# Softmax's 1e-9 by a sum over a pair, and the four-batch products spread over 18 steps with their loads later

## The chip, the cores and the metric

The kernel runs on one core of a Trainium2 chip. The metric is the device time of one execution in microseconds (us); the kernel before takes 1392.96 us (median of three runs, 1392.74 to 1393.12).

## The reference

Attention over 8 batches, 8 heads, 576 positions and head size 64, with 32 memory slots, and behind it a mixture of four dense experts over the 4608 resulting rows. All is float32.

```python
a = softmax(phi, over the 32 slots)              # per batch and head: 576 x 32
k_m, v_m = a^T k, a^T v                          # 32 x 64
scores = (q k_m^T) / sqrt(64)
scores = scores - max(scores); attn = exp(scores)
attn = attn / (sum(attn) + 1e-9)                 # the 1e-9 that is changed
x = (attn v_m), heads side by side               # 4608 x 512
p = domain_probs / (sum(domain_probs) + 1e-9)
out = sum over e of p[:, e] * (relu(x w1[e]) w2[e])   # w1: 512 x 1024, w2: 1024 x 512
```

## The kernel before

Every float32 matrix is split into a high and a low part, and a product is three TensorE passes (high·high, high·low, low·high). x itself is never formed: `v_m` is multiplied into `w1` first ("vw", 256 x 1024 for a batch and an expert), and `relu(attn · vw)` is the hidden layer.

Batches go in pairs ("groups" k = 0 to 3). For k = 0 and 1 the work runs in steps numbered s: 128 steps (`PAIR`) for a group, 32 (`STEPS`) for each of its four experts, the first 16 for the even batch (odd = 0) and the others for the odd one. Each 16 are two halves of the batch's rows by eight chunks j of the hidden layer. A step calls, in this order, `accumulate()`, `run_plan(s)`, `first(s + 2)` and `second(s)`. `first` (lines 641 to 643) multiplies `attn` by vw for the step after next; it reads tile `vw[k, e, odd, j // 4, g]`, g = 0 and then 1, so chunks 0 to 3 need the pieces with fh = 0 and chunks 4 to 7 those with fh = 1. `second` (lines 674 to 676) multiplies the hidden chunk by `w2`. From step 256 (`BEGIN`) on, groups 2 and 3 run in another form (`unit`, line 1002).

`run_plan(s)` emits what the tables at the top of the file put at step s: splits of weights, parts of the attention of later batches, and these:

- `units_four`: for expert e and half fh it computes the rows of vw for four batches at once (`four_mm`, line 579), splits the result into a tile `vst` (line 584 on ScalarE, 585 on VectorE; a ring of three buffers, `KVS`) and stores it to memory as `vwd` from GpSimd's queue (`to_memory`, line 567). `FOUR_AT[fh][hp]` is the step, counted from the start of the expert before, at which the weights of pair hp are taken; its two products follow 2 and 3 steps later (`FOUR_LAG`). The table serves the fourth expert (e = 3) of batches 0 to 3, computed in steps 64 to 95, and the first (e = 0) of batches 4 to 7, in steps 224 to 255.
- `load_vw` (line 618): eight transfers of 128 KB on SyncE's (SP's) queue bring the pieces with one (odd, fh) of one expert back from memory. `VW_LOAD_AT[odd][fh]` is its step. It serves e = 3 of group 0, loaded from step 64 on, and of group 1, loaded from step 192 on.
- `load_w2` (line 186): in groups after the first the split `w2` comes back from memory, one chunk j of 512 KB per step from step 24 of the expert before (`W2_AGAIN`). Chunk j goes into the buffer that `second` leaves one chunk earlier.
- `write_v` (line 448): eight small transfers on SP that copy a batch's v into `vs`; for batch 7 in step 220.

Steps up to 36 are ordered by the compiler's scheduler; from step 36 each engine and each queue keeps the order in which the code emits its work. SP's queue is in order: a transfer whose wait isn't met holds all behind it.

The softmax of `attn` is `soft` (lines 490 to 493), 24 calls, all on VectorE: a sum over 32 slots, an addition of 1e-9, a reciprocal and the multiplication.

Of the kernel before, what the change touches and what calls it, by code (L numbers as in the profile page):

```python
# [9 lines left out]
F32 = mybir.dt.float32  # L10
# [3 lines left out]
AX = mybir.AxisListType  # L14
# [3 lines left out]
B, H, S, D, M = 8, 8, 576, 64, 32  # L18
N, DM, E, F = 4608, 512, 4, 1024
P = 128  # L20
# [12 lines left out]
AHEAD = 2  # L33

FREE = 36
VW_LOAD_AT = ((20, 25), (28, 32))
TURN = (0, 2, 1, 3)

FOUR = (3, 0)

FOUR_AT = ((6, 8, 10, 12), (14, 16, 18, 20))
FOUR_LAG = 2


# [39 lines left out]
def body(ctx: ExitStack, tc: tile.TileContext, qm, qt, kv, kvt, phi, prob, w1, w1d, w2, out):  # L84
    nc = tc.nc
    pool = lambda name, **k: ctx.enter_context(tc.tile_pool(name=name, bufs=1, **k))
    const, wp, work, att = pool("const"), pool("wp"), pool("work"), pool("att")
# [18 lines left out]
    def give(ps):  # L106
        tag, n, _ = lent.pop(id(ps))
        idle[tag].append(n)
# [4 lines left out]
    vts = [const.tile([P, NP, 2, P], F32R, name=f"vt{i}") for i in range(2)]  # L113
    for t in [vts[0].bitcast(F32)] + kT + [vts[1].bitcast(F32)]:
        nc.gpsimd.memset(t, 0.0)
    pt = const.tile([P, N // P, E], F32, name="pt")
    hm = work.tile([P, NJ, 2, P], F32R, name="hm")

# [136 lines left out]
    st = {}  # L255
# [196 lines left out]
    def tiles(t0):  # L452
        return (2, P) if t0 < 4 else (1, 64)
# [14 lines left out]
    def scores_max(b, t0):  # L468
        nt, n = tiles(t0)
        sc = st["sc", b, t0]  # L470
        scv = sc.rearrange("p i a (h m) -> p (i a h) m", m=M)[:n, :nt * H, :]
        mx = att.tile([P, 2 * H, 1], F32, name="mx", tag="mx", bufs=2)
        nc.vector.tensor_reduce(mx[:n, :nt * H, 0], scv, AX.X, ALU.max)
        at = att.tile([P, nt * H, M], F32, name="at", tag=f"at{t0}")
        av = at[:n, :nt * H, :]
        nc.vector.tensor_sub(av, scv, mx[:n, :nt * H].broadcast_to([n, nt * H, M]))
        give(sc)
        st["at", b, t0] = at

    def scores_exp(b, t0):  # L480
        nt, n = tiles(t0)
# [3 lines left out]
    def soft(b, t0):  # L485
        nt, n = tiles(t0)
        av = st["at", b, t0][:n, :nt * H, :]
        z = att.tile([P, 2 * H, 1], F32, name="z", tag="z", bufs=2)
        zv = z[:n, :nt * H]
        nc.vector.reduce_sum(zv[:, :, 0], av, AX.X)  # L490
        nc.vector.tensor_scalar_add(zv[:, :, 0], zv[:, :, 0], 1e-9)
        nc.vector.reciprocal(zv[:, :, 0], zv[:, :, 0])
        nc.vector.tensor_mul(av, av, zv.broadcast_to([n, nt * H, M]))

# [3 lines left out]
    def unit_scores(b, t0):  # L498
        def emit(q):
            scores_mm(b, t0, q)  # L500
            scores_max(b, t0)
            scores_exp(b, t0)
            soft(b, t0)
        return q_key(b, t0), emit
# [107 lines left out]
    def load_vw(k, e, odd, fh):  # L612
        b = 2 * k + odd
        for g in range(2):
            t = vw_tile(k, e, odd, fh, g)
            for h in range(4):
                r = slice(M * slot(b, h), M * slot(b, h) + M)
                nc.sync.dma_start(t[r].bitcast(F32), vwd[b // 4, e, fh, g, h][r])
# [85 lines left out]
    def at(s, unit):  # L704
        plan[s].append(unit if isinstance(unit, tuple) else (None, unit))
# [32 lines left out]
    def attention(b, s, written, scores, turns):  # L738
# [27 lines left out]
        for t0, n in zip((0, 2, 4), scores):  # L766
            at(n, (q_key(b, t0), lambda q, t0=t0: scores_mm(b, t0, q)))
            at(n + 1, lambda t0=t0: scores_max(b, t0))
            at(n + 2, lambda t0=t0: scores_exp(b, t0))
            at(n + 3, lambda t0=t0: soft(b, t0))  # L770
# [11 lines left out]
    for k in range(NG):  # L782
        for e in range(E):
# [19 lines left out]
            for fh in range(2):  # L803
                when, gap = (FOUR_AT_7, 2) if s >= BEGIN else (FOUR_AT, 1)
                for hp in range(NP if by_four and nk % 2 == 0 else 0):
# [4 lines left out]
                for odd in range(2 if by_four else 0):  # L810
                    when = VW_LOAD_AT if nk < SEVEN else VW_LOAD_7
                    at(s + when[odd][fh], lambda a=(nk, ne, odd, fh): load_vw(*a))
# [309 lines left out]
    with tc.manual_schedule():  # L1122
# [54 lines left out]
        kv_pick(0, 1)  # L1177
        scores_mm(0, 0, q, (2, 3))
        scores_max(0, 0)
        split_w1(w1g[0], 0, 1, gps)  # L1180
        write_vt_0(0, slice(1, 2))
# [4 lines left out]
        scores_exp(0, 0)  # L1186
        vw_out(pv[0], 0, 0, 0, 0, (0,))
        soft(0, 0)
        keep_warm(3)
        for hp in (1, 2):  # L1190
# [83 lines left out]
```

## Time and profile before

| | |
|---|---|
| time, median of 3 runs | 1392.96 us |
| profiled execution | 1392.14 us, span of its instructions 1390.3 us |
| PE (TensorE matmul) busy | 1362.0 us (98%) |
| DVE (VectorE) busy | 841.3 us (61%) |
| ACT (ScalarE) busy | 625.4 us (45%) |
| POOL (GpSimd) busy | 617.4 us (44%) |
| mean granted TensorE clock | 0.997 of full speed |
| HBM traffic over the span | 215 GB/s |

In the rows of the profile a number at the start is the time in us since the span began, the next one the duration; then come engine, line and operation, what is written `<-` what is read, and in square brackets how long the engine idled ahead of it and what ended that. Of a merged row (x4) the duration is that of all of them. SPq and POOLq are the queues from which these engines issue transfers.

### The profile page before, as it was taken

How to read it: one execution, taken by the hardware profiler on the slowest of the kernel's cores; microseconds unless marked ns; L12 is line 12 of the kernel's file. 1: busy time of each engine (PE TensorE's matmuls, PEld its weight loads, DVE VectorE, ACT ScalarE, POOL GpSimd, SP SyncE). 2: the span in 40 equal slices, each digit the busy share in tenths (PEclk: the TensorE clock that was granted, in tenths of full speed). 3: DMA queues.
4: the chain of work that ended last, by engine and by line, in shares of the span. 5: the costliest groups of instructions: out<-in, count | busy, mean ns of one | idle time of the engine just before them, and what ended most of it. 6: DMA issues, size and time to landing. Idle time of an engine off the chain costs nothing.

```text
span 1390.3 us, 25223 instructions
## 1 busy us (share of the span) xinstructions
PE 1362.0 (98%) x8894; PEld 1248.4 (90%) x8894; DVE 841.3 (61%) x1894; ACT 625.4 (45%) x1536; POOL 617.4 (44%) x652
## 2 busy tenths in 40 slices
PE   7999999999999999999999999999999999999998
PEld 6788888788888888889888998999999999999998
DVE  7875535446755365454434467777767666666666
ACT  6765555443345465463344354555543333333332
POOL 4400354745353424433144375677753334443432
PEclk9999999999999999999999999999999999999999
DMA  6742354897675364354598898899984866666661
GB/s 255 240 165 76 117 182 173 311 322 240 210 281 212 107 229 146 125 203 143 178 290 296 277 321 292 286 344 311 326 298 131 259 186 177 180 173 175 175 181 75
DMA packets 102029, 301.37 MB, mean 217 GB/s; under 512 B 24976, under 2 KB 26128, under 8 KB 101904
## 3 DMA queue, kind: packets, MB, share of 16 engines
q1 hardware_dynamic: 81168, 224.26, 51.9%
q0 software_dynamic: 19584, 71.31, 13.0%
q10 hardware_dynamic: 1152, 4.19, 0.7%
q8 instruction: 71, 1.16, 0.3%
q14 instruction: 54, 0.44, 0.1%
HBM read 213.46 MB, written 84.93 MB: 215 GB/s over the span
## 4 chain that ended last, share of the span: by engine, by line
PE 89%; DVE 4%; DMA 2%; issue 2%; ACT 1%; SPq 0%; POOL 0%; DVEq 0%; ACTq 0%; POOLq 0%
PE banks L1002 22%; PE banks L676 9%; PE banks L674 9%; PE banks L675 9%; PE banks L916 5%; PE banks L917 5%; PE banks L918 5%; PE banks L641 5%; PE banks L642 4%; PE banks L643 4%; PE banks L579 3%; PE banks L463 2%; PE banks L357 2%; DMA stage<-in_w 1%; PE banks L1040 1%
## 5 line engine op out<-in xcount | busy, mean ns | idle before, releaser
L1020 DVE SCALAR_TENSOR_TENSOR acc<-banks,pt,acc 128x256 f32<-128x256 f32 x416 | 200.0, 481 | 107.7 <-PE banks L1002 104.2
L160 POOL TENSOR_TENSOR w<-stage,w 128x512 fp32r<-128x512 f32 x134 | 177.0, 1332 | 188.7 <-ACT w L159 179.4
L655 DVE SCALAR_TENSOR_TENSOR h<-banks,h 128x256 fp32r<-128x256 f32 x256 | 107.3, 420 | 168.6 <-ACT h L653 111.4
L676 PE MATMUL banks<-w,h 128*128 128x512 f32 x512 | 201.2, 393 | 3.4 <-DVE h L655 3.4
L674 PE MATMUL banks<-w,h 128*128 128x512 f32 x512 | 201.9, 394 | 0.1
L675 PE MATMUL banks<-w,h 128*128 128x512 f32 x512 | 201.4, 393 | 0.0
L653 ACT ACTIVATE h<-banks 128x256 fp32r<-128x256 f32 x256 | 98.0, 384 | 199.8 <-PE banks L643 169.9
L641 PE MATMUL banks<-AT,vw 128*128 128x256 f32 (+1 forms) x512 | 156.6, 306 | 3.7 <-DVE h L655 1.8
L1002 PE MATMUL banks<-w,a 128*128 128x256 f32 x1080 | 154.4, 282 | 0.3 <-DVE acc L1020 0.2
L643 PE MATMUL banks<-AT,vw 128*128 128x256 f32 (+1 forms) x512 | 150.9, 295 | 1.2 <-DVE vw L556 1.2
L916 PE MATMUL banks<-AT,vw 128*128 128x256 f32 (+1 forms) x512 | 151.6, 296 | 0.0
L642 PE MATMUL banks<-AT,vw 128*128 128x256 f32 (+1 forms) x512 | 151.3, 296 | 0.0
L917 PE MATMUL banks<-AT,vw 128*128 128x256 f32 (+1 forms) x512 | 151.1, 295 | 0.0
L918 PE MATMUL banks<-AT,vw 128*128 128x256 f32 (+1 forms) x512 | 150.9, 295 | 0.0
L1002 PEld LDWEIGHTS banks<-w,a 128*128 128x128 f32 x1080 | 143.6, 188 | 4.8 <-issue 0.9
L983 POOL TENSOR_TENSOR vt<-ph,vt 128x512 fp32r<-128x512 f32 x64 | 84.1, 1314 | 107.3 <-ACT vt L982 78.3
L676 PEld LDWEIGHTS banks<-w,h 128*128 128x128 f32 x512 | 96.3, 188 | 25.8 <-DVE h L655 4.3
L346 POOL TENSOR_TENSOR kvs<-stage,kvs 128x512 fp32r<-128x512 f32 x58 | 75.4, 1317 | 93.2 <-ACT kvs L345 87.3
L641 PEld LDWEIGHTS banks<-AT,vw 128*128 128x128 f32 x512 | 96.8, 189 | 13.8 <-DVE vw L556 3.8
L674 PEld LDWEIGHTS banks<-w,h 128*128 128x128 f32 x512 | 96.4, 188 | 12.0 <-ACT h L653 0.4
L675 PEld LDWEIGHTS banks<-w,h 128*128 128x128 f32 x512 | 96.4, 188 | 10.9
L159 ACT CAST w<-stage 128x512 fp32r<-128x512 f32 x168 | 102.7, 619 | 4.5 <-DMA stage<-in_w 2.1
(149 smaller groups left out, 2985.4 us busy)
## 6 DMA issues: line engine op xcount, KB each, us to landing
w<-kw SPq DMA_DIRECT2D x93, 512.0 KB, 5.5
vwd<-vst POOLq DMA_DIRECT2D x80, 512.0 KB, 6.4
vw<-vwd SPq DMA_DIRECT2D x320, 128.0 KB, 6.0
w<-v SPq DMA_DIRECT2D x55, 512.0 KB, 5.6
stage<-in_w SPq DMA_DIRECT2D x44, 512.0 KB, 4.5
stage<-in_w1d SPq DMA_DIRECT2D x40, 512.0 KB, 5.3
stage<-in_kv SPq DMA_DIRECT2D x32, 512.0 KB, 4.3
kw<-w POOLq DMA_DIRECT2D x24, 512.0 KB, 5.6
```

What stands on the lines that cost most here:

```text
L160: eng.tensor_sub(dst[:, 1, :], raw, dst[:, 0, :].bitcast(F32))
L641: nc.tensor.matmul(ps, w[:, 0, f], at_t[:, g, 0, c], start=g == 0, stop=False)
L642: nc.tensor.matmul(ps, w[:, 0, f], at_t[:, g, 1, c], start=False, stop=False)
L643: nc.tensor.matmul(ps, w[:, 1, f], at_t[:, g, 0, c], start=False, stop=g == 1)
L674: nc.tensor.matmul(po[t], x[:, 0, :], w[:, 0, :], start=j == 0, stop=False)
L675: nc.tensor.matmul(po[t], x[:, 0, :], w[:, 1, :], start=False, stop=False)
L676: nc.tensor.matmul(po[t], x[:, 1, :], w[:, 0, :], start=False, stop=j == NJ - 1)
L916: nc.tensor.matmul(ps, w[:, 0, f], at_t[:, g, 0, c], start=g == 0, stop=False)
L917: nc.tensor.matmul(ps, w[:, 0, f], at_t[:, g, 1, c], start=False, stop=False)
L918: nc.tensor.matmul(ps, w[:, 1, f], at_t[:, g, 0, c], start=False, stop=g == 1)
L1002: nc.tensor.matmul(ps, a[:, l, jj], w[:, r, c], start=start and jj + i == 0, stop=jj == 1 and i == 2, skip_group_check=True,)
L1020: VE.scalar_tensor_tensor(a, src, p, a, ALU.mult, ALU.add)
```

## The change

```diff
-VW_LOAD_AT = ((20, 25), (28, 32))
+VW_LOAD_AT = ((20, 29), (28, 36))
...
-FOUR_AT = ((6, 8, 10, 12), (14, 16, 18, 20))
+FOUR_AT = ((6, 8, 10, 13), (15, 17, 20, 22))
...
+    guarded = const.tile([P, 2 * H, 2], F32, name="guarded")
+    nc.gpsimd.memset(guarded[:, :, 1], 1e-9)
...
-        st["at", b, t0] = at
+        st["at", b, t0], st["mx", b, t0] = at, mx
...
-        z = att.tile([P, 2 * H, 1], F32, name="z", tag="z", bufs=2)
-        zv = z[:n, :nt * H]
-        nc.vector.reduce_sum(zv[:, :, 0], av, AX.X)
-        nc.vector.tensor_scalar_add(zv[:, :, 0], zv[:, :, 0], 1e-9)
+        zv = st["mx", b, t0][:n, :nt * H]
+        nc.vector.reduce_sum(guarded[:n, :nt * H, 0], av, AX.X)
+        nc.vector.reduce_sum(zv[:, :, 0], guarded[:n, :nt * H], AX.X)
         nc.vector.reciprocal(zv[:, :, 0], zv[:, :, 0])
         nc.vector.tensor_mul(av, av, zv.broadcast_to([n, nt * H, M]))
```

The addition of 1e-9 becomes a second sum, over the pair (sum, 1e-9), into the tile that held the maximum. The sixteen products of one expert, one per step over 16 steps before, now have one step free behind the sixth and one behind the twelfth. Both loads of the pieces with fh = 1 come four steps later. The lines of the changed file are numbered two higher from line 115 or so on, and one higher behind `soft`.

The first place is SP's queue around step 217 to 222, where group 1 gets its fourth expert. `vwd` + five digits is a stored piece: batch set 0, expert 3, fh, g, and the head within g; `kw3j` is chunk j of the fourth expert's `w2`. Before:

```order
L186 DMA w2_6846<-kw31_3987 128x1024
L618 DMA vw_6848<-vwd03100_2966 32x1024
...
L618 DMA vw_6853<-vwd03113_3186 32x1024
L186 DMA w2_6881<-kw32_4013 128x1024
L186 DMA w2_6901<-kw33_4036 128x1024
L186 DMA w2_6918<-kw34_4067 128x1024
L618 DMA vw_6920<-vwd03000_2737 32x1024
...
L618 DMA vw_6925<-vwd03013_2934 32x1024
L448 DMA vs_5331<-vh_6883 64x2x32 x8
L186 DMA w2_6955<-kw35_4086 128x1024
L186 DMA w2_6977<-kw36_4108 128x1024
```

And after:

```order
L188 DMA w2_6830<-kw31_3977 128x1024
L188 DMA w2_6855<-kw32_4003 128x1024
L188 DMA w2_6875<-kw33_4026 128x1024
L188 DMA w2_6892<-kw34_4057 128x1024
L619 DMA vw_6894<-vwd03000_2733 32x1024
...
L619 DMA vw_6899<-vwd03013_2950 32x1024
L450 DMA vs_5320<-vh_6857 64x2x32 x8
L188 DMA w2_6929<-kw35_4076 128x1024
L619 DMA vw_6931<-vwd03100_2982 32x1024
...
L619 DMA vw_6936<-vwd03113_3212 32x1024
L188 DMA w2_6961<-kw36_4098 128x1024
```

The eight loads of the even batch's fh = 1 pieces stood ahead of chunk 2 of `w2`; now they stand behind chunk 5, the eight loads of the odd batch's fh = 0 pieces and the eight writes of `vs`.

The second place is PE's order in step 226, in which `first(228)` reads those pieces. Before:

```order
L676 MATMUL banks_72<-w2_6846,h_7010 128x512
L641 MATMUL banks_72<-AT_3431,vw_6848 128x256 [waits DMAHW6_49,DMAHW7_49,DMAHW5_49,DMAHW0_49]
L642 MATMUL banks_72<-AT_3431,vw_6848 128x256
L643 MATMUL banks_72<-AT_3431,vw_6848 128x256
L641 MATMUL banks_72<-AT_3431,vw_6853 128x256 [waits DMAHW3_49,DMAHW4_49,DMAHW2_49,DMAHW1_49]
```

And after:

```order
L677 MATMUL banks_72<-w2_6830,h_6994 128x512
L642 MATMUL banks_72<-AT_3416,vw_6931 128x256 [waits DMAHW3_49,DMAHW4_49,DMAHW2_49,DMAHW1_49]
L643 MATMUL banks_72<-AT_3416,vw_6931 128x256
L644 MATMUL banks_72<-AT_3416,vw_6931 128x256
L642 MATMUL banks_72<-AT_3416,vw_6936 128x256 [waits DMAHW6_49,DMAHW7_49,DMAHW5_49,DMAHW0_49]
```

PE's order has not moved: the matmul stands behind the `w2` chunk of step 225 in both, and waits for the four transfers of each tile.

The third place is VectorE's order around `soft` for batch 2, in step 98. Before:

```order
L655 SCALAR_TENSOR_TENSOR h<-banks,h 128x256 x2
L490 TENSOR_REDUCE z<-at 128x16
L491 TENSOR_SCALAR z<-z 128x16
L492 RECIPROCAL z<-z 128x16
L493 TENSOR_TENSOR at<-at,z 128x512
L655 SCALAR_TENSOR_TENSOR h<-banks,h 128x256 x2
```

And after:

```order
L656 SCALAR_TENSOR_TENSOR h<-banks,h 128x256 x2
L491 TENSOR_REDUCE guarded<-at 128x16
L492 TENSOR_REDUCE mx<-guarded 128x16
L493 RECIPROCAL mx<-mx 128x16
L494 TENSOR_TENSOR at<-at,mx 128x512
L656 SCALAR_TENSOR_TENSOR h<-banks,h 128x256 x2
```

One operation changes its kind; its place in the queue, ahead of the split of the hidden layer (`h`), stays. In steps up to 36 the scheduler, which counts the operations' costs, has also ordered a number of rows otherwise on every engine.

## The prediction

> **What bounds the kernel now.** I read the page first, then PE's waits, then the time lines of PE, VectorE, GpSimd and SP at the places where PE waits and where the change moves work.
>
> ```profile
> PE 1362.0 (98%) x8894; PEld 1248.4 (90%) x8894; DVE 841.3 (61%) x1894; ACT 625.4 (45%) x1536; POOL 617.4 (44%) x652
> PE 89%; DVE 4%; DMA 2%; issue 2%; ACT 1%; SPq 0%; POOL 0%; DVEq 0%; ACTq 0%; POOLq 0%
> ```
>
> PE is busy for 98% of the span and holds 89% of the chain that ended last. Its matmuls do not change, so the change can only pay or cost where PE waits: 28.3 us in all (1390.3 - 1362.0). Of PE's waits these are the longest behind the start:
>
> ```profile
> PE banks L676 <- DVE h L655: 3.4, 2, 2.0
> PE banks L579 <- ACT h L653: 2.5, 1, 2.5
> ```
>
> The columns are us in total, how often, and the longest. The 2.0 us is tied to the softmax, the 2.5 us to the four-batch products; I take each in turn, then the moved loads.
>
> **The sum over a pair.** All 24 additions of 1e-9, and three rows of the one that matters:
>
> ```profile
> L491 DVE TENSOR_SCALAR z<-z x24: 152/175/5192, 27.8 to 1062.7; 128x16 f32<-128x16 f32 x16, 64x8 f32<-64x8 f32 x8
> L490 DVE TENSOR_REDUCE z<-at x24: 399/676/686, 27.1 to 1062.3; 128x16 f32<-128x512 f32 x16, 64x8 f32<-64x256 f32 x8
> 334.44 5.19 DVE L491 TENSOR_SCALAR z<-z 128x16 f32<-128x16 f32 x1
> 334.10 5.49 POOL L160 TENSOR_TENSOR w<-stage,w 128x512 fp32r<-128x512 f32 x4
> 341.63 0.50 PE L676 MATMUL banks<-w,h 128*128 128x512 f32 x1 [2.03 <-DVE h L655]
> ```
>
> Sixteen numbers per partition take 175 ns as a rule, and 5192 ns once: from 334.44 to 339.63, while GpSimd ran four subtractions back to back until 339.59. The hidden layer's split stood behind it on VectorE, and PE idled 2.03 us for it. The sum in its place costs, by the two shapes of the other sums (399 ns for 256 elements, about 680 for 512: some 1.1 ns an element over about 120 ns), about 155 ns for 32 elements: 24 times nothing gained or lost. A sum over 512 elements never took over 686 ns in 24 executions, however busy GpSimd was, so I let the new one not wait. That removes PE's 2.03 us. Next in line is the multiplication, which reads two operands from SBUF; it has waited for GpSimd too:
>
> ```profile
> 850.78 1.68 DVE L493 TENSOR_TENSOR at<-at,z 128x512 f32<-128x512 f32 x1
> ```
>
> 1.68 us is its longest, so it slips in after one GpSimd operation. At 334.9 it would end by about 336.6 instead of 340.6, and the split in time. Term: -2.0 us (bounds: -2.0, and -0.3 if it waits as the addition did).
>
> The Trainium skill, SBUF — State Buffer, section Who interferes with whom, says that `tensor_scalar` can take a mode that needs the port pair shared with GpSimd, that `tensor_reduce` on trn2 never does, and that a two-input operation from SBUF contends with GpSimd's reads. The rows agree on the first two; by the third the wait could move to the multiplication, which is the second rival below.
>
> The constant's memset stands on GpSimd's queue at the start behind others and ahead of 3.8 us of idle time there; its cover is that idle time, and without it it would cost a fraction of a us. 0.
>
> **The products in 18 steps.** The wait of 2.5 us:
>
> ```profile
> 261.16 1.10 POOL L567 DMA_DIRECT2D vwd<-vst  x1
> 270.19 0.58 ACT L584 CAST vst<-banks 128x512 fp32r<-128x512 f32 x1 [7.52 <-DMA vwd<-vst]
> 271.65 0.47 PE L579 MATMUL banks<-w,vs 128*128 128x512 f32 x1 [2.53 <-ACT h L653]
> 272.40:275.80 3.40, 3.09 (x10) 2.80 (x11) 1.87 (x5) 2.29 (x7) 3.36 (x5) 0.50 0.64 123
> 275.90:279.30 3.40, 3.40 (x19) 2.94 (x18) 0.33 (x2) 0.60 (x2) 0.95 (x2) 1.00 1.01 401
> ```
>
> ACT waits 7.52 us for the first store, issued at 261.16, because the ring holds three pieces and this is the fourth. PE then stops ahead of the sixth product. The first six products keep their steps (6, 8 and 10 in the table are unchanged); the free steps come behind them. So this wait stays, with its price: 2.53 us and 3.4 us in which TensorE had half its clock (0.50 in the first window row, 1.00 in the next), worth 1.7 us. From there to 334 us PE does not wait, and it does not between 597 and 861 us, where the table's other use lies, so the free steps have nothing to remove. Sixteen products of two matmuls are the same work wherever they stand. Their stores end two steps later, which matters only to the loads below. Term: 0 (bounds -0.5 and +1, the size of PE's small waits).
>
> **The moved loads, first use (step 93).** `first(100)` in step 98 needs them.
>
> ```profile
> 318.01 0.35 SPq L145 DMA_DIRECT2D stage<-in_w  x1
> 334.45 0.28 PE L641 MATMUL banks<-AT,vw 128*128 128x256 f32 x1
> 313.48 4.14 SPq L618 DMA_DIRECT2D vw<-vwd  x8
> L618 SPq DMA_DIRECT2D vw<-vwd x320: 302/419/1489, 289.3 to 1331.9; - x160
> DMA to landing us min/median/max: 2.3/6.0/9.7
> ```
>
> SP now issues them behind the weights' load that went out at 318.01. Eight loads take SP 4.1 us (313.48) to about 6 and land 6.0 us after issue: 318.4 + 5.2 + 6.0 = 329.6, against a need at 334.45. Hidden, by 5 us. Ahead of it the last store must land, two steps later than before, at about 321. Term: 0.
>
> **The moved loads, second use (step 221).** Here steps take 2.1 us only:
>
> ```profile
> 688.40 0.28 PE L641 MATMUL banks<-AT,vw 128*128 128x256 f32 x1
> 700.96 0.28 PE L641 MATMUL banks<-AT,vw 128*128 128x256 f32 x1
> 701.32 0.28 PE L641 MATMUL banks<-AT,vw 128*128 128x256 f32 x1
> 709.31 0.31 PE L641 MATMUL banks<-AT,vw 128*128 128x320 f32 x1
> ```
>
> At 709.31 the width turns to 320: that is `first(232)`, step 230. Back by 2.09 us a step, step 226 begins at 700.96, where `first(228)` needs the tile with g = 0, and at 701.32 the one with g = 1; 688.40 is step 220. SP's queue meanwhile:
>
> ```profile
> 682.28 0.33 SPq L186 DMA_DIRECT2D w<-kw  x1
> 682.65 4.22 SPq L618 DMA_DIRECT2D vw<-vwd  x8
> 687.20 1.72 SPq L186 DMA_DIRECT2D w<-kw  x3
> 688.97 6.52 SPq L618 DMA_DIRECT2D vw<-vwd  x8
> 695.80 4.66 SPq L448 DMA_DIRECT2D vs<-vh  x6
> 699.50 2.67 SPq L448 DMA_DIRECT2D vs<-vh  x3
> 702.26 1.64 SPq L186 DMA_DIRECT2D w<-kw  x3
> 703.95 6.18 SPq L618 DMA_DIRECT2D vw<-vwd  x8
> ```
>
> (The two `vs` rows overlap by one of the eight.) Before, the loads in question went out at 682.65. In the new order they stand behind chunk 5 of `w2`, so behind everything down to 702.26. SP cannot run ahead of this: chunk 4 waits for the buffer that step 219 leaves at 688.4, and the queue after it is bound by its transfers. Worked out:
>
> - the odd batch's eight loads from 688.97: between 4.14 and 6.52 us; 1 MB less is under way ahead of them than before, so I take 4.2: 693.2
> - eight `vs` writes: 6.4 us before (695.80 to 702.2), at least eight times their shortest:
>
> ```profile
> L448 SPq DMA_DIRECT2D vs<-vh x64: 590/606/1420, 28.9 to 701.2; - x64
> ```
>
>   or 4.7; I take the middle, 5.6: 698.8
> - chunk 5: 0.4: 699.2
> - the eight loads: between 4.14 and 6.18, taken as 5.2: the last goes out by 704.4 and lands 6.0 later, at 710.4. The fourth, which ends the wait for g = 0, lands at 699.2 + 2.6 + 6.0 = 707.8.
>
> PE stops at 700.96 until 707.8, does three matmuls, and stops again until 710.4: 710.4 - 701.3 = 9.1 us. The least is 688.97 + 4.1 + 4.7 + 0.3 + 4.1 + 2.3 (the shortest landing) = 704.5, a loss of 3.2; the most is the old position, 702.6 + 6.2 + 9.7 = 718.5, a loss of 17.2. Both ends are past the need. A stop like this should halve the clock as the one of 2.53 us did: 3.4 us at 0.50 cost 1.7 (bounds 0 and 2.6, one and a half such stretches). The Trainium skill, TensorE: Matmul & The Clock Gate, Part 1, asks for an idle window of about 3.4 us before the clock drops; in the trace 2.53 us sufficed, and the measurement decides; a stop of 9 us meets either.
>
> Behind the stop PE has what it needs: chunks 6 and 7 go out after the loads but are due 8 us later than before, and the odd batch's other eight loads are due in step 242. Term: +9.1 + 1.7 = +10.8.
>
> **The scheduled steps up to 36.** PE waits there, as in
>
> ```profile
> 37.17 0.50 PE L676 MATMUL banks<-w,h 128*128 128x512 f32 x1 [1.37 <-DVE h L655]
> 49.87 0.39 PE L643 MATMUL banks<-AT,vw 128*128 128x256 f32 x1 [0.82 <-DVE vw L556]
> ```
>
> and rows change places around it. No row tells which way; the waits from 33 us on (1.37 + 0.82 and smaller) bound a gain at 2.6, a loss is taken as large. Term: 0.
>
> **Sum**: -2.0 + 9.1 + 1.7 = +8.8 us on the profiled execution of 1392.14 us (1.8 above its span) gives 1400.9. The median of the runs is 0.8 above that execution, 1392.96; on it 1401.8 us.
>
> **Rivals.**
> 1. The loads come in time after all (other side). Place: SP's queue from 688.4 to 701. It decides at the point where all eight have landed by 701.3, so the last must go out by about 695.3, before SP had begun the `vs` writes in the old trace (695.80). Speaking for it: the queue holds 1 MB less ahead of them. Against: even the shortest rows give 704.5. Then only the softmax counts: 1392.96 - 2.0 = 1391.0; with 0.8 us or more from the scheduled steps it would be faster by over 0.2% (2.8 us, about what a measurement tells from no change).
> 2. The loads are late and the softmax's wait moves to the multiplication, held until 339.6 as the addition was. For it: it has two inputs from SBUF, and 1.68 us shows that it waits. Against: in 24 executions it never waited for more than one operation. It ends 0.3 us earlier than before: 1401.8 + 1.7 = 1403.5.
> 3. The first use is late too: decided by SP reaching it 5 us later than 318.4. 3 us more: 1404.8.
>
> **Chances.** Forecast 0.70, rival 1 0.13, rival 2 0.12, rival 3 0.05. The range for 8 in 10: the low end, 1396.5, is the forecast with SP some 5 us quicker than taken; the high end, 1407, takes in rivals 2 and 3 and a loss of 14 us at step 226. Rival 1 lies outside below. Faster: 0.04 (rival 1 with luck at the start). Within 0.2%: 0.09 from rival 1 and 0.02 from the forecast's low tail, whose least sum is 3.2 - 2.0 = +1.2. Slower: 0.85.
>
> **What would show it.** In the trace after: no addition over GpSimd's chain near 334 us and no PE idle time at 341; the wait at 271 us as before, half clock behind it; PE idle at about 699 (701 less the 2.0) on its vw matmul, released by transfers `vw<-vwd`, in two pieces of some 7 and 2.5 us, and a window of clock 0.50; the eight loads leaving SP behind the `vs` writes, near 699 to 705. Wrong it would be if SP passed the `vs` writes before 692, if step 226 took other tiles than those, or if the start moved by more than 3 us.

## The result and the profile after

The changed kernel takes 1407.15 us (median of six runs, 1403.07 to 1408.55) against 1393.04 (1391.14 to 1395.85) for the kernel before on the same chip: a ratio of 1.0092, 95% interval 1.0077 to 1.0106, so 12.8 us slower by the ratio. The execution that the profile shows took 1405.31 us, its span 1403.4 us. The page's engine row, its chain of work that ended last, the clock in 40 slices, and the longest of PE's waits:

```profile
PE 1364.9 (97%) x8894; PEld 1250.5 (89%) x8894; DVE 836.8 (60%) x1894; ACT 625.5 (45%) x1536; POOL 618.0 (44%) x653
PE 87%; DVE 5%; DMA 3%; issue 2%; ACT 2%; POOL 1%; SPq 1%; ACTq 0%; DVEq 0%; POOLq 0%
PEclk9999999999999999999989999999999999999999
PE banks L642 <- DMA vw<-vwd: 10.0, 2, 8.9
PE banks L677 <- DVE h L656: 5.0, 3, 2.0
PE banks L580 <- ACT h L654: 0.7, 1, 0.7
```

PE's busy time grew by 2.9 us only (1364.9 - 1362.0), the time in which it is idle by 10.2. A wait for transfers `vw<-vwd` that was not there before, 10.0 us in two pieces, stands at the top, and one slice of the clock is no longer full. With the matmuls of both traces laid side by side by their place in PE's order (times of the kernel before), the changed kernel is 1.5 us behind at 46 us, 3.5 at 95 and 3.3 at 269; it is level again at 280 and still level at 700, 13.1 behind past step 226, and 13.2 at the end.

**Step 226.** SP's queue, PE, two windows (length, PE busy, PEld, DVE, ACT, POOL, then granted clock, share of DMA, GB/s), and the first matmul of `first(232)`:

```profile
682.31 6.64 SPq L188 DMA_DIRECT2D w<-kw  x4
689.00 4.88 SPq L619 DMA_DIRECT2D vw<-vwd  x8
693.98 6.36 SPq L450 DMA_DIRECT2D vs<-vh  x8
700.43 0.54 SPq L188 DMA_DIRECT2D w<-kw  x1
701.02 7.29 SPq L619 DMA_DIRECT2D vw<-vwd  x8
710.02 0.56 PE L642 MATMUL banks<-AT,vw 128*128 128x256 f32 x1 [8.87 <-DMA vw<-vwd]
712.15 0.58 PE L642 MATMUL banks<-AT,vw 128*128 128x256 f32 x1 [1.15 <-DMA vw<-vwd]
703.20:706.60 3.40, 0.00 (x0) 0.00 (x0) 0.00 (x0) 0.00 (x0) 0.00 (x0) 0.50 1.01 275
710.00:716.80 6.80, 5.63 (x18) 4.78 (x19) 0.42 (x1) 0.38 (x1) 0.00 (x0) 0.50 0.98 265
722.39 0.31 PE L642 MATMUL banks<-AT,vw 128*128 128x320 f32 x1
```

The loads that PE needs at 701.2 (710.02 - 8.87) leave SP from 701.02 to 708.31, behind the odd batch's loads and the eight `vs` writes. While PE is idle the clock falls to 0.50, and it is still 0.50 when PE is back: 5.63 us of work at half clock cost 2.8 us. The first matmul of `first(232)`, at 709.31 us in the profile before, starts at 722.39, so this place costs 13.1 us; the waits and the half clock are 12.8 of them.

**The softmax near 335 us.** The sum over the pair, GpSimd's four subtractions, the multiplication and PE:

```profile
334.52 0.18 DVE L492 TENSOR_REDUCE mx<-guarded 128x16 f32<-128x32 f32 x1
334.61 5.51 POOL L162 TENSOR_TENSOR w<-stage,w 128x512 fp32r<-128x512 f32 x4
335.03 5.65 DVE L494 TENSOR_TENSOR at<-at,mx 128x512 f32<-128x512 f32 x1
341.67 0.50 PE L677 MATMUL banks<-w,h 128*128 128x512 f32 x1 [1.98 <-DVE h L656]
```

The new sum does not wait. The multiplication behind it does, until GpSimd's chain is through, and PE idles 1.98 us where it idled 2.03.

**The products near 271 us.** GpSimd's first store, ScalarE's fourth split, and PE's sixth product:

```profile
264.42 1.09 POOL L568 DMA_DIRECT2D vwd<-vst  x1
271.64 0.58 ACT L585 CAST vst<-banks 128x512 fp32r<-128x512 f32 x1 [5.72 <-DMA vwd<-vst]
273.09 0.47 PE L580 MATMUL banks<-w,vs 128*128 128x512 f32 x1 [0.70 <-ACT h L654]
```

ScalarE went on 7.2 us after the issue of the store that it waits for (264.42 to 271.64), where it was 9.0 before (261.16 to 270.19). PE waits 0.70 us instead of 2.53, and the clock does not fall. The first use of the moved loads is hidden: SP issues them from 317.87 to 322.6, and PE does not wait for them.

### The profile page after: what moved, and what is told of

It reads as the page before. It is cut to its first block, busy times and chain, and to the rows that moved or that the text cites. A ratio compares the mean times of both kernels' runs of the same rounds, so it can differ in the third digit from the quotient of the medians.

```text
span 1403.4 us, 25226 instructions
## 1 busy us (share of the span) xinstructions
PE 1364.9 (97%) x8894; PEld 1250.5 (89%) x8894; DVE 836.8 (60%) x1894; ACT 625.5 (45%) x1536; POOL 618.0 (44%) x653
## 4 chain that ended last, share of the span: by engine, by line
PE 87%; DVE 5%; DMA 3%; issue 2%; ACT 2%; POOL 1%; SPq 1%; ACTq 0%; DVEq 0%; POOLq 0%
PE banks L1003 22%; PE banks L677 8%; PE banks L676 8%; PE banks L675 8%; PE banks L917 5%; PE banks L918 5%; PE banks L919 5%; PE banks L642 4%; PE banks L643 4%; PE banks L644 4%; PE banks L580 2%; PE banks L359 2%; PE banks L465 2%; DVE vw L557 1%; PE banks L1041 1%
```

## The experiments

The kernels of the first four ran together beside the kernel before at 1393.08 us, the next four beside 1393.22, the last two beside 1394.24; all are medians, and ratios are to those.

**1. The kernel before, with only the second use's loads later.** `VW_LOAD_AT` gets a pair for each expert so served; `nk` is 0 for group 0 and 1 for group 1.

```diff
-VW_LOAD_AT = ((20, 25), (28, 32))
+VW_LOAD_AT = (((20, 25), (28, 32)), ((20, 29), (28, 36)))
...
-                    when = VW_LOAD_AT if nk < SEVEN else VW_LOAD_7
+                    when = VW_LOAD_AT[nk] if nk < SEVEN else VW_LOAD_7
```

> The kernel before, with the four-step delay of the loads with fh = 1 for the second use alone (the fourth expert of group 1). Theory A (the loads stand behind the vs writes in SP's queue and reach step 226 too late; PE waits about 10 us and then works 4.7 us at half clock): 12 to 14 us slower than before, about 1406, with PE waiting 8 to 10 us on transfers vw<-vwd near 701 us. Theory B (the loss comes mostly from the start and the scheduled steps, which the softmax reorders, and the wait at step 226 is a part): 5 us slower or less.

Measured: 1407.89 us, ratio 1.0096 (1.0078 to 1.0113). PE around step 226, from that trace:

```profile
712.59 0.55 PE L641 MATMUL banks<-AT,vw 128*128 128x256 f32 x1 [6.86 <-DMA vw<-vwd]
715.00 0.58 PE L641 MATMUL banks<-AT,vw 128*128 128x256 f32 x1 [1.43 <-DMA vw<-vwd]
```

Both loads with fh = 1 of group 1 move, sixteen transfers; PE waits for the even batch's eight. This move alone makes the whole loss (1.0096 against 1.0092); side by side this place costs 11.8 us.

**2. The changed kernel, with the second use's loads back.**

```diff
-VW_LOAD_AT = ((20, 29), (28, 36))
+VW_LOAD_AT = (((20, 29), (28, 36)), ((20, 25), (28, 32)))
...
-                    when = VW_LOAD_AT if nk < SEVEN else VW_LOAD_7
+                    when = VW_LOAD_AT[nk] if nk < SEVEN else VW_LOAD_7
```

> The changed kernel, with the old load steps for the second use alone. Theory A: no wait at step 226, so 1392 to 1396, the kernel before within what differs at the start (+3.5 us in the profile) and at the four-batch products (-3.6 us). Theory B: it stays over 1400.

Measured: 1393.88 us, ratio 1.0005 (0.9991 to 1.0018); PE does not wait between 690 and 725 us. All that is left of the change, the sum over the pair, the 18 steps and the first use's later loads, comes to nothing that the interval (-1.3 to +2.5 us) tells from zero.

**3. Only the sum over the pair.** The kernel before with the edits of the softmax as in the change.

> The kernel before, with the sum over a pair alone. Theory A (the wait for GpSimd passes to the multiplication behind it): no gain, 1393 within 2 us, the multiplication of 5 to 6 us and PE's wait of 2 us near 341 us still there. Theory B (the multiplication was held by chance in the one profile): a normal multiplication of 0.7 to 1.7 us there and 1391. Theory C (the new order of the scheduled steps costs): 1396 or more, with the loss before 95 us.

Measured: 1396.05 us, ratio 1.0011 (1.0000 to 1.0023). No gain; the median is 3.0 us above that of the kernel before, more than Theory A's 2, and the interval just touches 1. The multiplication in that trace:

```profile
334.60 5.67 DVE L494 TENSOR_TENSOR at<-at,mx 128x512 f32<-128x512 f32 x1
```

It is held in both traces, so this is no chance of one execution, and PE idles 2.01 us behind it. Theory C, a loss in the scheduled steps, isn't excluded: this trace has one too (see the scheduled steps below).

**4. Only the products in 18 steps, with the first use's loads later.**

```diff
-VW_LOAD_AT = ((20, 25), (28, 32))
+VW_LOAD_AT = (((20, 29), (28, 36)), ((20, 25), (28, 32)))
...
-FOUR_AT = ((6, 8, 10, 12), (14, 16, 18, 20))
+FOUR_AT = ((6, 8, 10, 13), (15, 17, 20, 22))
...
-                    when = VW_LOAD_AT if nk < SEVEN else VW_LOAD_7
+                    when = VW_LOAD_AT[nk] if nk < SEVEN else VW_LOAD_7
```

> The kernel before, with the products in 18 steps and the later loads that they need for the first use, and the old loads for the second. Theory A (the wait at 271 us comes ahead of the free steps, and its size changes from run to run): 1393 within 2 us, a wait ahead of the sixth product of 0.5 to 3 us. Theory D (the free steps do remove it): 1389, without that wait.

Measured: 1394.26 us, ratio 1.0004 (0.9990 to 1.0019). The wait ahead of the sixth product, from the list of PE's waits and from ScalarE's rows:

```profile
PE banks L579 <- ACT h L653: 2.7, 1, 2.7
271.69 0.59 ACT L584 CAST vst<-banks 128x512 fp32r<-128x512 f32 x1 [7.73 <-DMA vwd<-vst]
```

It is as long as before, and 2.2 us in experiment 2, which has the 18 steps too; in experiment 3, which has not, it is 1.3. The wait follows the time from the store's issue to ScalarE's split: 9.2 us here, 8.8 in experiment 2, 7.9 in experiment 3, 7.2 in the profile of the changed kernel. So the 0.70 us there came with a quicker store in that one execution, not with the 18 steps.

**5. The changed kernel, with batch 7's `vs` writes four steps later,** so that the eight loads pass them on SP's queue.

```diff
-        at(written + 2, lambda: write_v(b, b < 4))
+        at(written + (6 if b == 7 else 2), lambda: write_v(b, b < 4))
```

> The changed kernel, with the eight writes of batch 7's v to vs four steps later (224, not 220), so that in SP's queue they stand behind the late loads instead of ahead. Theory A (the loads wait for their turn in SP's queue): the 6.4 us that the writes held the queue fall away, PE's wait at step 226 drops from 10.0 to about 4 us, and the time to 1398 to 1401. Theory E (the transfer engines are full there, and the order matters little): the wait drops by less than 2 us, and the time stays over 1404.

Measured: 1400.99 us, ratio 1.0055 (1.0039 to 1.0071), 6.2 us less than the changed kernel. SP and PE:

```profile
691.87 4.26 SPq L619 DMA_DIRECT2D vw<-vwd  x8
696.36 0.34 SPq L188 DMA_DIRECT2D w<-kw  x1
696.88 5.50 SPq L619 DMA_DIRECT2D vw<-vwd  x8
704.09 8.68 SPq L450 DMA_DIRECT2D vs<-vh  x8
704.95 0.36 PE L642 MATMUL banks<-AT,vw 128*128 128x256 f32 x1 [0.93 <-DMA vw<-vwd]
707.69 0.39 PE L642 MATMUL banks<-AT,vw 128*128 128x256 f32 x1 [2.15 <-DMA vw<-vwd]
```

Nothing of the loads themselves changed, only what stands ahead of them. The wait falls from 10.0 to 3.1 us (0.93 + 2.15); the difference of 6.9 is about what the eight writes held the queue for (6.36). Side by side this place costs 5.2 us instead of 13.1; that the medians differ by 6.2 and not by 7.9 stays open. The 3.1 us that are left fit the odd batch's loads, which still stand ahead (4.26 us), but no run takes these away.

**6. Experiment 1 with the eight late loads issued from ScalarE's queue.**

```diff
-                nc.sync.dma_start(t[r].bitcast(F32), vwd[b // 4, e, fh, g, h][r])
+                (nc.scalar if (k, odd, fh) == (1, 0, 1) else nc.sync).dma_start(t[r].bitcast(F32), vwd[b // 4, e, fh, g, h][r])
```

> The kernel before with the late loads of the second use, as in the run that was 0.96% slower, but the eight late ones issued from ACT's queue in the same step 221. Theory A: ACT reaches them within about 2 us of step 221 (690.5 us) and they land by about 701, so PE waits 0 to 2 us at step 226, and the time is 1392 to 1396. Theory E: with as many bytes under way they land as late as on SP's queue, and PE waits 5 us or more.

Measured: 1398.61 us, ratio 1.0031 (1.0019 to 1.0043). The time was missed. PE does not wait for the loads any more, but ScalarE, which computes on the same instruction stream, is held while it issues them:

```profile
690.49 7.07 ACTq L618 DMA_DIRECT2D vw<-vwd  x8
697.65 0.62 ACT L213 CAST sv<-raw 128x512 fp32r<-128x512 f32 x1 [6.80 <-DMA vw<-vwd]
698.60 0.50 PE L674 MATMUL banks<-w,h 128*128 128x512 f32 x1 [1.95 <-ACT h L653]
```

PE loses 2.5 us there (1.95, and 0.54 more at 711.95) for the 8.3 of experiment 1. That is about half of the 5.4 us by which the medians differ. The profiled execution, at 1396.28 us, is one of the quicker of its twelve, and no other wait of it accounts for the rest, which stays open.

**7. The kernel before, with the softmax that meets GpSimd's chain at step 100 instead of 98.** The 1e-9 is added as before.

```diff
-            at(n + 3, lambda t0=t0: soft(b, t0))
+            at(n + (5 if (b, t0) == (2, 2) else 3), lambda t0=t0: soft(b, t0))
```

> The kernel before, with the softmax of batch 2's second pair of tiles in step 100, not 98, and nothing else. Theory A (an operation that needs the port shared with GpSimd waits out GpSimd's chain of four subtractions near 334 to 340 us, whichever operation it is): in step 100 the chain is over, no softmax operation takes more than 1.7 us, PE's wait of 2.0 us near 341 goes, and the time falls by 2 to 3.7 us to about 1390. Theory F (the hidden layer's split is late there for another reason): the wait of 2 us stays in place.

Measured: 1392.29 us, ratio 0.9987 (0.9976 to 0.9997). The addition there:

```profile
339.39 1.07 DVE L491 TENSOR_SCALAR z<-z 128x16 f32<-128x16 f32 x1
```

GpSimd's chain runs from 334.89 to 340.42 us here, so the addition meets the last of its four operations and waits for that one only; PE's 2.0 us at 341 are gone. The median gains 0.9 us (interval 0.4 to 3.3), less than the 2 to 3.7 expected; the prediction's price of 2.0 lies in the interval, but isn't settled by it. The sum over a pair was not the way to collect it.

**8. The kernel before, with both free steps ahead of the wait of 2.5 us.** Both come behind the second product, and only the first use's loads are later.

```diff
-FOUR_AT = ((6, 8, 10, 12), (14, 16, 18, 20))
+FOUR_AT = ((6, 10, 12, 14), (16, 18, 20, 22))
...
-VW_LOAD_AT = ((20, 25), (28, 32))
+VW_LOAD_AT = (((20, 29), (28, 36)), ((20, 25), (28, 32)))
...
-                    when = VW_LOAD_AT if nk < SEVEN else VW_LOAD_7
+                    when = VW_LOAD_AT[nk] if nk < SEVEN else VW_LOAD_7
```

> The kernel before, with two free steps among the sixteen products, both behind the second product (ahead of the stall at 271 us) in place of behind the sixth and twelfth, the later loads for the first use that this needs, and the old loads for the second use. Theory A (the fourth piece waits for the first store, which lands 9 us after issue): the fourth result comes two steps later, ACT's wait of 7.5 us shrinks to 2 us or less, PE's wait ahead of the sixth product goes, and the time falls by 1 to 4 us to about 1390. Theory G (the stores are late because the products before are late): the wait moves along.

Measured: 1388.83 us, ratio 0.9964 (0.9950 to 0.9978). ScalarE still waits for the first store, but no longer long enough to stop PE:

```profile
269.41 0.59 ACT L584 CAST vst<-banks 128x512 fp32r<-128x512 f32 x1 [2.31 <-DMA vwd<-vst]
```

**9. Experiments 7 and 8 together.**

> The kernel before with two edits: the four-batch products spread to 6, 10, 12, 14 and 16, 18, 20, 22 with the first use's loads of the third expert's pieces moved by as much and the second use's loads as in before; and the softmax of the second pair put off to step 100, where the 1e-9 is added as before. Theory A (each wait stands at a place of its own on TensorE): the gains add. The spread products alone gave a ratio of 0.9964, the put-off softmax alone 0.9987, so about 0.995, 1387 us (1384 to 1389); no wait of TensorE over 1 us at 271 and at 341. Theory B (the gains overlap, because the put-off softmax falls among products that now come later): 0.9965, about 1389 us, with a wait of about 2 us on an activation left between 335 and 350.

Measured: 1386.51 us (five runs, 1384.82 to 1388.12), ratio 0.9945 (0.9931 to 0.9959), where the two ratios multiply to 0.9951: the gains add. Its engine row, and windows around the matmuls ahead of which the kernel before waits at 271 and 341 (here near 270 and 336):

```profile
PE 1360.9 (98%) x8894; PEld 1248.2 (90%) x8894; DVE 837.1 (60%) x1894; ACT 625.9 (45%) x1536; POOL 617.4 (45%) x652
270.00:273.40 3.40, 3.40 (x20) 3.01 (x19) 1.25 (x3) 1.61 (x5) 1.99 (x4) 1.00 1.01 413
335.00:338.40 3.40, 3.40 (x27) 2.81 (x26) 2.51 (x5) 0.38 (x1) 1.22 (x1) 1.00 0.45 146
```

PE is busy throughout at full clock in both.

**10. Experiment 9, with batch 5's attention stage starting two steps earlier,** for the wait of 1.83 us near 516 that it causes on VectorE.

```diff
-    5: (PAIR + 26, PAIR + 53, (PAIR + 76, PAIR + 80, PAIR + 84), (PAIR + 112, PAIR + 113, PAIR + 114)),
+    5: (PAIR + 24, PAIR + 53, (PAIR + 76, PAIR + 80, PAIR + 84), (PAIR + 112, PAIR + 113, PAIR + 114)),
```

> As the kernel with both edits, and the attention stage that begins two steps into the second pair's list begins two steps earlier, so that the normalisation which waits behind split weights on VectorE near 516 us falls elsewhere. Theory A (the 1.8 us wait of TensorE near 516 is that stage's queue on VectorE): it goes, 2 to 3.5 us less than without the third edit (1.8 us, and 1.7 more in the executions in which the clock is halved there), about 1384 us. Theory B (VectorE is as full two steps earlier): the wait moves by about 6 us or so and the time is the same within 1.5 us.

Measured: 1394.32 us, ratio to the kernel before 1.0002 (0.9991 to 1.0014); all that experiment 9 had gained is lost. PE in the kernel of experiment 9, then in this one:

```profile
510.80 0.58 PE L641 MATMUL banks<-AT,vw 128*128 128x256 f32 x1 [1.83 <-DVE h L655]
```

```profile
498.69 0.39 PE L641 MATMUL banks<-AT,vw 128*128 128x256 f32 x1 [0.54 <-DVE zs L279]
502.81 0.39 PE L641 MATMUL banks<-AT,vw 128*128 128x256 f32 x1 [1.17 <-DVE vw L556]
507.82 0.39 PE L641 MATMUL banks<-AT,vw 128*128 128x256 f32 x1 [2.07 <-DVE vw L556]
548.49 0.30 PE L514 MATMUL banks<-ident,at 64*128 64x64 f32 x2 [2.09 <-DVE at L493]
```

The wait of 1.83 us became one of 2.07 three us earlier, others grew beside it, and a new one of 2.09 stands at 548, with half clock behind it. Between 440 and 600 us PE's waits add up to 7.4 us for 3.0. Theory B held in that the wait moved; that it would grow neither theory had said. The medians differ by 7.8 us, the profiled executions by 4.9 only (1393.04 and 1388.12), because this one was 2.7 us ahead when it reached 490. Side by side it loses 7.7 us between 490 and 600: 4.4 in waits and 1.7 by the half clock at 548; the other 1.6 are not accounted for.

## Why the prediction came out as it did

The direction and the place were right. The sum of the prediction, +8.8, stands against +13.2 in the profiled executions. On the prediction's 1392.96 us the measured ratio gives 1405.8, inside its range (1396.5 to 1407) near the high end; the median of 1407.15 is just above it. By its terms:

**The second use: right in mechanism, place and order; short by 2.3 us.** Forecast were two stops of some 7 and 2.5 us at step 226, released by `vw<-vwd` behind the `vs` writes; they are 8.87 and 1.15. Experiments 1, 2 and 5 show the place and the queue. The `vs` writes took 6.36 us (taken as 5.6), the eight loads 7.29 (taken as 5.2), and the landing made up for 2 us of it: PE went on at 712.15, 3.8 us after the last load had left. So the wait is 10.0 for 9.1. The half clock cost 2.8 and not 1.7: the stop is long enough that the clock was still low for 6.8 us from PE's first return at 710.0, not for 3.4. The bound given was 2.6. These two, 0.9 and 1.1, are 2.0 of the 2.3.

**The softmax's -2.0: the step that failed.** It let the multiplication slip in after one operation of GpSimd, because 1.68 us was its longest time in 24 executions. Those 24 did not test it: at this place the addition ahead of it had waited out the chain in its stead. The second rival, given 0.12, is what happened: 5.65 us where the addition had 5.19, and PE's wait unchanged. The Trainium skill, SBUF — State Buffer, section Who interferes with whom, states that a two-input operation from SBUF contends with GpSimd's reads. The trace agrees, 5.65 and 5.67 us in two kernels; the size of it, four operations of GpSimd and not one, is from these traces.

**The products in 18 steps: 0, right.** Experiment 4 measures 1.0004. That the free steps stand behind the wait and not ahead of it was the reason given; experiment 8, which puts both ahead, gains 4.4 us (1393.22 - 1388.83), close to the 2.53 + 1.7 that the wait and its half clock were priced at.

**The first use: 0, right.** Experiments 2 and 4 contain it and show no wait for the loads.

**The scheduled steps: 0 in the sum, +3.5 in the trace; 2.0 of it fit the change.** Rows at the start of the changed kernel:

```profile
11.68 2.08 PE L359 MATMUL banks<-kvs,a 128*128 128x256 f32 x8 [3.31 <-DVE a L311]
66.37 0.62 ACT L161 CAST w<-stage 128x512 fp32r<-128x512 f32 x1 [2.19 <-DMA stage<-in_w]
68.35 0.44 PE L379 MATMUL banks<-ident,xs 128*128 128x128 f32 x2 [1.47 <-ACT xs L370]
```

The first of PE's waits was 1.93 us in the profile before. In experiment 6, which has neither the sum nor other products, it is 3.1 us, so this one, and the 1.5 us by which the changed kernel is behind at 46, vary from execution to execution. The second is another matter. ScalarE waits for a weight's transfer and hands PE its copy late; between 46 and 95 us this kernel falls back by 2.0 us. The same stretch costs 1.9 to 2.0 in experiments 2, 3 and 5, the other kernels with the sum and its order of the scheduled steps. Of the seven other experiments' traces six lose nothing there; one, experiment 9, loses 1.6 with the same waits in the old order. So the new order seems to make the late transfer likely; the traces are few, and why it does stays open. The prediction had put the term at 0 because no row told which way, and had named a start moved by more than 3 us as a sign of being wrong; that sign came.

Against this stand the -3.4 at 271, a matter of one execution (experiment 4). The prediction had not foreseen that this wait could be nearly absent from a single trace; that it cancels the start is luck.

Summed up: 8.8 + 2.0 (softmax) + 2.3 (second use) + 3.5 (start) - 3.4 (271) is the 13.2.

## What to carry to other kernels

A transfer that is issued four steps later is late by everything that its in-order queue has put ahead of it in those steps, so the rows of that queue decide, not the landing time of the transfer. An operation that waits for a neighbour's chain can be replaced by one that does not, and nothing is gained if the next in line then waits for the same chain; moving the group to the chain's end took PE's wait away. And free steps helped ahead of the wait that they were to fill, and did nothing behind it.

## What was not expected of the hardware

A multiplication with both operands in SBUF, 0.69 us in experiment 9, took 5.65 us in the changed kernel: it ended after the whole of GpSimd's four back-to-back operations (334.61 to 340.12), and did not slip in between two of them. At 850.78 us in the profile before, the row of 1.68 us, it seems to have done so: it ended at 852.46, while the second of two GpSimd operations in a row went from 851.87 to 853.61. What makes the difference is not shown. A wait as short as 2 us can halve TensorE's clock in one execution and not in another. PE idles 2.0 us ahead of the same matmul in experiments 2 and 3, at 344.9 and at 341.3 us; the window behind it, of experiment 2 and then of experiment 3:

```profile
345.00:348.40 3.40, 3.40 (x14) 2.44 (x15) 0.53 (x2) 0.00 (x0) 0.00 (x0) 0.51 1.01 348
```

```profile
341.30:344.70 3.40, 3.40 (x22) 2.73 (x23) 0.84 (x3) 0.39 (x1) 0.00 (x0) 1.00 0.39 143
```

14 matmuls in the one and 22 in the other. Three such waits, at 271, 341 and 516, each followed by half clock worth 1.7 us in some executions and not in others, can make several us of the spread of the kernel before (1389.21 to 1397.83 in 29 runs); how much of it they make was not shown.
